# The first MLP layer's half-used products as pairs of 64 rows, and six PSUM banks in a fixed turn

## The chip, the cores and the metric

One core of a Trainium2 chip runs the whole program. The metric is the device time of one execution in microseconds. The kernel before took 1213.66 us, the median of three runs (1213.50 to 1214.83). The engines have short names in the profile: PE is TensorE (matmuls; PEld its weight loads), DVE is VectorE, ACT is ScalarE, POOL is GpSimd, and SP the engine that only issues DMAs here.

## The reference: what is computed

```
# x: 8 batches of 4224 tokens of 192 values; weight: 8 heads of 7 taps
w = softmax(weight over the 7 taps)
x = causal convolution along the tokens, 7 taps, one set of taps per head of 24 values
X = fft over tokens, then over the 192 values
u = x + real(X)
un = (u - mean(u)) / sqrt(var(u) + 1e-6)            # over the 192 values
out = u + max(un @ w_ch1, 0) @ w_ch2                # 192 -> 768 -> 192
```

All of it is fp32. The kernel carries each fp32 operand of a matmul as two fp16 parts, hi and lo, and adds three products, hi x hi, hi x lo and lo x hi.

## The kernel before, in words

**Stages.** Each batch goes through a chain of stages. `conv_unit` does the convolution with banded matrices into PSUM tiles `pc` and stores the rows to DRAM (`store_rows`); in later batches `split_windows` first makes hi and lo parts, with a small matmul `pn` for the scale. `load_x` and `split_x` bring the rows back and split them into XH and XL. `stage_a` and `stage_b` do the Fourier transform in two factors (tiles `pa` and `pb`), and `prep` the last factor (tile `pq`), which it adds to the residual `u` that `load_res` has gathered. `prep` goes on with mean, variance and normalisation, the last parts of it on GpSimd, and writes the fp16 halves `hl`. `transposes` turns `hl` into `kt` with one transposing DMA from SP. Then come the two MLP layers, `mlp_hidden` and `mlp_out`, and `store_out`.

**Steps.** The MLP works in steps of 512 tokens. A batch has nine steps, `it` 0 to 7 with 512 tokens and the short one `Q0` (`it` 8) with 128. The loop at L1127 runs over all 72 steps, numbered n. In step n it traces the hidden units of step n, the output groups of step n - 1 (four of 128 tokens), the store of step n - 2, the end of `prep` and the transpose for step n + 2, the start of `prep` for step n + 3 and gathers for n + 5. The earlier stages of the next batches are called fills. `spread` puts them evenly between these units; `stage_a` of the next batch falls into its steps `it` 3 and 4, `stage_b` mostly into 5 to 8, 0 and 1, the convolution of the batch after that into 3 to 6, and the loads and splits into 7, 8, 0, 1 and 2.

**The first layer.** The 192 inputs are 128 + 64. `W1` has four blocks of 128 rows: index 0 is the hi part of rows 0 to 127, index 1 their lo part, index 2 the hi part of rows 128 to 191, and index 3 their lo part. The 64 rows of indices 2 and 3 stand twice, in the lower and in the upper half of the partitions (`mirror_tail`). `kt` has three blocks of 128 rows: hi of 0 to 127, then hi of 128 to 191 above lo of 128 to 191, then lo of 0 to 127. For each of six tiles of 128 hidden values, L884 adds five products of 128 rows and 512 tokens:

```
order = ((0, 0), (1, 0), (0, 2), (2, 1), (3, 1))     # (block of W1, block of kt)
```

In the last, lo weights meet hi values in one half of the rows, which is needed, and lo values in the other half. L888 (ScalarE) takes relu of the tile to `hh`, and L889 (VectorE) takes the fp16 remainder to `hlo`.

**The second layer.** `mlp_out` adds 18 matmuls of 192 columns a group of 128 tokens (L903, L906, L909) into `po`, and L915 adds the result to `u`.

**PSUM.** Eight banks are three pools: tag "f" with four banks for pa, pb, pc, pq and pn, tag "h" with two for the hidden tiles `ph`, and tag "o" with two for `po`. Within a pool, a tile takes a bank that is free.

**What sets the order.** The code is written out as one stream; a planner then orders each engine's instructions ahead of time, earlier traced first among those that it takes to be ready. `after(x)` and `issue_after` put an instruction behind another on the same engine; `in_turn` puts one behind the last relu. On the chip each engine's queue keeps that order.

## Time and profile before

| | |
|---|---|
| median of three runs | 1213.66 us (1213.50 to 1214.83) |
| profiled execution, its own time | 1214.54 us |
| span of the profile, first to last instruction | 1212.7 us |
| busy PE, DVE, POOL, ACT | 1155.2, 891.5, 810.6, 637.2 us |
| mean granted clock of TensorE | 0.98 |
| chain that ended last, share of PE | 86% |

All durations come from one execution. Consecutive matmuls overlap in the records, so that their durations add up to more than the time they take; the distance from one start to the next is what counts. "Idle before" of a group is the time for which its engine did nothing just ahead of it, with what ended it.

### The profile page before, as it was taken

How to read it: one execution, taken by the hardware profiler on the slowest of the kernel's cores; microseconds unless marked ns; L12 is line 12 of the kernel's file. 1: busy time of each engine (PE TensorE's matmuls, PEld its weight loads, DVE VectorE, ACT ScalarE, POOL GpSimd, SP SyncE). 2: the span in 40 equal slices, each digit the busy share in tenths (PEclk: the TensorE clock that was granted, in tenths of full speed). 3: DMA queues.
4: the chain of work that ended last, by engine and by line, in shares of the span. 5: the costliest groups of instructions: out<-in, count | busy, mean ns of one | idle time of the engine just before them, and what ended most of it. 6: DMA issues, size and time to landing. Idle time of an engine off the chain costs nothing.

```text
span 1212.7 us, 31442 instructions
## 1 busy us (share of the span) xinstructions
PE 1155.2 (95%) x12736; PEld 913.9 (75%) x12736; DVE 891.5 (74%) x2124; ACT 637.2 (53%) x1020; POOL 810.6 (67%) x1104
## 2 busy tenths in 40 slices
PE   4279999989999999999999999999999999999998
PEld 4178768867878778787877878787787878787766
DVE  7657686787867977688777978679777887566543
ACT  5547566555655556655655655555555554333222
POOL 0217875399747897389954997479963899677940
PEclk9589999989999999999999999999999999999999
DMA  8945856366565647474663956556474643333221
GB/s 307 257 119 149 219 166 147 110 170 122 150 162 141 145 122 182 133 173 115 152 170 100 200 117 175 137 146 167 114 179 124 160 104 76 89 65 92 69 56 43
DMA packets 238370, 170.56 MB, mean 141 GB/s; under 512 B 119369, under 2 KB 221969, under 8 KB 238225
## 3 DMA queue, kind: packets, MB, share of 16 engines
q1 hardware_dynamic: 184744, 109.95, 37.3%
q10 hardware_dynamic: 46952, 45.24, 13.6%
q0 software_dynamic: 6528, 13.38, 4.4%
q8 instruction: 99, 1.62, 0.6%
q14 instruction: 47, 0.38, 0.1%
HBM read 83.82 MB, written 58.55 MB: 117 GB/s over the span
## 4 chain that ended last, share of the span: by engine, by line
PE 86%; DVE 5%; DMA 4%; ACT 2%; issue 2%; SPq 1%; ACTq 0%; another core or an unknown queue 0%; DVEq 0%
PE ph L884 33%; PE po L903 10%; PE po L909 10%; PE po L906 10%; PE pa L619 6%; PE pq L769 6%; PE pb L672 5%; PE pc L468 4%; PE pa L646 1%; DMA xs<-sc 1%; PE pc L473 1%; DMA xs_yl<-sc 1%; DMA XL<-in_w_dram 1%; ACT XH L594 1%; DVE hlo L889 1%
## 5 line engine op out<-in xcount | busy, mean ns | idle before, releaser
L884 PE MATMUL ph<-kt,W 128*128 128x512 f16 (+1 forms) x2160 | 497.7, 363 | 6.4 <-DVE hlo L889 6.3
L888 ACT ACTIVATE hh<-ph 128x512 f16<-128x512 f32 (+1 forms) x400 | 236.6, 593 | 354.7 <-PE ph L884 336.8
L909 PE MATMUL po<-W,hlo 128*128 128x192 f16 x1584 | 384.5, 246 | 0.0
L903 PE MATMUL po<-W,hh 128*128 128x192 f16 x1584 | 384.4, 246 | 0.1
L906 PE MATMUL po<-W,hh 128*128 128x192 f16 x1584 | 384.1, 246 | 0.0
L889 DVE SCALAR_TENSOR_TENSOR hlo<-ph,hh 128x512 f16<-128x512 f32 (+1 forms) x400 | 269.0, 676 | 117.6 <-ACT hh L888 114.6
L884 PEld LDWEIGHTS <-W 128*128 128x128 f16 x2160 | 192.4, 98 | 142.6 <-issue 9.4
L824 POOL TENSOR_SCALAR un<-u,mv,y 128x192 f32<-128x192 f32 x260 | 274.9, 1065 | 7.8
L718 POOL DMA_INDIRECT u<-sc,rows_sb x136 | 154.5, 1136 | 31.4 <-issue 30.8
L903 PEld LDWEIGHTS <-hh 128*128 128x128 f16 x1584 | 154.8, 98 | 24.0 <-issue 0.3
L906 PEld LDWEIGHTS <-hh 128*128 128x128 f16 x1584 | 154.7, 98 | 21.4 <-issue 0.5
L909 PEld LDWEIGHTS <-hlo 128*128 128x128 f16 x1584 | 154.8, 98 | 19.7 <-issue 0.3
L841 POOL TENSOR_TENSOR hl<-un,hl 128x512 f16<-128x512 f32 (+2 forms) x142 | 129.3, 932 | 5.6
L787 DVE SCALAR_TENSOR_TENSOR u<-pq,g,u 128x128 f32<-128x128 f32 (+1 forms) x328 | 102.9, 380 | 28.5 <-PE pq L769 24.5
L815 POOL TENSOR_SCALAR v<-mv 128x4 f32<-128x4 f32 (+1 forms) x71 | 20.1, 282 | 145.7 <-DVE mv L795 128.2
L602 DVE SCALAR_TENSOR_TENSOR XL<-xs,s_x,XH 128x768 f16<-128x768 f32 (+1 forms) x56 | 93.2, 1664 | 22.9 <-ACT XH L594 22.9
L915 DVE SCALAR_TENSOR_TENSOR u<-po,fo,u 128x384 f32<-128x384 f32 (+1 forms) x136 | 81.1, 597 | 27.0 <-PE po L909 26.9
L594 ACT ACTIVATE XH<-xs,s_x 128x768 f16<-128x768 f32 (+1 forms) x56 | 94.3, 1686 | 9.1 <-DMA xs<-sc 9.0
L769 PE MATMUL pq<-c_sb,V 128*128 128x130 f16 (+1 forms) x1440 | 96.8, 215 | 0.1
L627 ACT ACTIVATE yh<-pa 99x512 f16<-99x512 f32 x112 | 65.2, 594 | 47.2 <-PE pa L619 40.3
L769 PEld LDWEIGHTS <-V 128*128 128x128 f16 (+1 forms) x1440 | 82.2, 100 | 8.3 <-issue 2.2
L619 PE MATMUL pa<-c_sb,XH 128*128 128x128 f16 x896 | 86.5, 219 | 0.0
(158 smaller groups left out, 1740.3 us busy)
## 6 DMA issues: line engine op xcount, KB each, us to landing
out_dram<-u SPq DMA_DIRECT2D x64, 384.0 KB
xt<-in_xw_dram ACTq DMA_DIRECT2D x30, 576.0 KB
sc<-xa ACTq DMA_DIRECT2D x30, 540.0 KB
xs<-sc SPq DMA_DIRECT2D x28, 288.0 KB
u<-sc SPq DMA_DIRECT2D x72, 96.0 KB
xt<-in_xw_dram SPq DMA_DIRECT2D x10, 576.0 KB
sc<-xa SPq DMA_DIRECT2D x10, 540.0 KB
xs<-sc SPq DMA_DIRECT2D x28, 192.0 KB
```

Source lines behind the costliest of these rows:

```text
L594: split = nc.scalar.activation(part(XH), src, AF.Copy, scale=bt.c)
L619: nc.tensor.matmul(pa[:, i], x[:, at], F[:, l], start=(n == 0), stop=(n == 2))
L718: nc.gpsimd.indirect_dma_start(to, None, bt.sc[:S], bass.IndirectOffsetOnAxis(ap=rows_sb[:, col : col + 1], axis=0),)
L769: mm = nc.tensor.matmul(po, weights(v, ND * r + k3), rhs[:, 0] if it == Q0 else rhs, start=(r + n == 0), stop=(r == 1 and n == 2),)
L824: (nc.vector if b + it == 0 else nc.gpsimd).tensor_scalar(un[:, g], u[:, g], mv[:, g, 0:1], y[:, g : g + 1], op0=ALU.subtract, op1=ALU.mult,)
L841: lower = (nc.vector if b + it == 0 else nc.gpsimd).tensor_tensor(bl[:, :, o : o + n], un[:, :ng, f], hi[:, :, f], op=ALU.subtract)
L884: nc.tensor.matmul(ph[:, n], W1[:, w, ht * 128 : (ht + 1) * 128], kt[:, k], start=(i == 0), stop=(i == len(order) - 1),)
L888: anchor[0] = nc.scalar.activation(hh, ph, AF.Relu).ins
L889: nc.vector.scalar_tensor_tensor(hlo, ph, 0.0, hh, op0=ALU.max, op1=ALU.subtract)
L903: nc.tensor.matmul(po[:, g % 2], hh[:, ht, tk], W2[:, ht, 0], start=(ht == 0), stop=False)
L906: nc.tensor.matmul(po[:, g % 2], hh[:, ht, tk], W2[:, ht, 1], start=False, stop=False)
L909: nc.tensor.matmul(po[:, g % 2], hlo[:, ht, tk], W2[:, ht, 0], start=False, stop=(ht == 5),)
```

## The change

It has three parts.

1. Banks. From the first step of batch 1 on, the four banks of "f" and the two of "h" are one list of six, and each new tile takes the next bank in a fixed turn (`psum`), whether that bank is the first to come free or not. Before that step, and for "o", the old groups remain, also in turn.
2. Paired steps. In the steps of the list `PAIRED` the fifth product is left out of the five. In its place `tails` traces, ahead of the step's other units, one matmul of 64 rows for each of the six tiles, with tile 5 first: even tiles use partitions 0 to 63 of `W1` and of `kt`, odd tiles partitions 64 to 127 of `W1` and a copy of the same 64 rows of `kt` (`bt.again`). Each of the six is put behind the one before it, and the first behind the last output matmul traced so far. `mlp_hidden_full` then adds the four other products to each bank, behind the tails. The order of units in a paired step is two hidden tiles, one output group, and so on; the last output group is kept to the end of the step, after all fills.
3. The copy. `repeat_tail` is one DMA from ScalarE's queue, traced in the step before a paired one, from `kt` to upper partitions of the memory of `band`, which is not used any more by then; four places are used in turn.

```
+    bank_sets = {"f": [0, 1, 2, 3], "h": [4, 5], "o": [6, 7]}
+    def psum(shape, tag, name):
+        k = bank_sets[tag].pop(0)
+        bank_sets[tag].append(k)
+        return ps.tile(shape, F32, tag=f"bank{k}", name=name)
...
-        pa = ps.tile([128, JT, 128], F32, tag="f", name=f"pa_{b}_{t}", bufs=4)
+        pa = psum([128, JT, 128], "f", f"pa_{b}_{t}")
...
+    spare = band.rearrange("p h t -> p (h t)").bitcast(F16).rearrange(
+        "p (k g t) -> p k g t", k=4, g=4
+    )
+    def repeat_tail(bt, it):
+        to = bt.again[it] = spare[64:, (bt.b * NIT + it) % 4]
+        with in_turn():
+            nc.scalar.dma_start(to, bt.kt[it][:64, 1])
+    def tails(bt, it):
+        b = bt.b
+        bt.h[it] = (
+            sb.tile([128, 6, 512], F16, tag="hh", name=f"hh_{b}_{it}"),
+            sb.tile([128, 6, 512], F16, tag="hlo", name=f"hlo_{b}_{it}"),
+        )
+        bt.ph[it] = [psum([128, 512], "h", f"ph_{b}_{it}_{ht}") for ht in range(6)]
+        behind = last_out[0]
+        for ht, ph in reversed(list(enumerate(bt.ph[it]))):
+            at = slice(64 * (ht % 2), 64 * (ht % 2) + 64)
+            with after(behind):
+                behind = nc.tensor.matmul(
+                    ph, W1[at, 3, ht * 128 : (ht + 1) * 128],
+                    bt.again[it] if ht % 2 else bt.kt[it][at, 1],
+                    start=True, stop=False,
+                ).ins
+        bt.behind = behind
+    def mlp_hidden_full(bt, it, ht):
+        ph, kt = bt.ph[it][ht], bt.kt[it]
+        hh, hlo = (h[:, ht] for h in bt.h[it])
+        with after(bt.behind):
+            for i, (w, x) in enumerate(((0, 0), (1, 0), (0, 2), (2, 1))):
+                nc.tensor.matmul(
+                    ph, W1[:, w, ht * 128 : (ht + 1) * 128], kt[:, x],
+                    start=False, stop=(i == 3),
+                )
+        anchor[0] = nc.scalar.activation(hh, ph, AF.Relu).ins
+        nc.vector.scalar_tensor_tensor(
+            hlo, ph, 0.0, hh, op0=ALU.max, op1=ALU.subtract
+        )
+        if ht == 5:
+            del bt.ph[it], bt.again[it]
...
-            nc.tensor.matmul(
+            last_out[0] = nc.tensor.matmul(
                 po[:, g % 2], hlo[:, ht, tk], W2[:, ht, 0],
                 start=False, stop=(ht == 5),
-            )
+            ).ins
...
+    PAIRED = [
+        n for n, (bt, it) in enumerate(steps)
+        if n >= NIT and it != Q0 and (bt.b == B - 1 or it in (0, 2, 3, 4, 6) and n > NIT)
+    ]
     for n in range(len(steps) + 1):
...
+        paired = n in PAIRED
+        if paired:
+            hid = [call(mlp_hidden_full, bt, it, ht) for ht in range(6)]
         out = []
         if prev:
             out = [call(mlp_out, *prev, g) for g in range(1 if prev[1] == Q0 else 4)]
         main = []
         while hid or out:
-            if hid:
-                main.append(hid.pop(0))
-            if out:
-                main.append(out.pop(0))
+            for units in (hid, hid, out) if paired else (hid, out):
+                if units:
+                    main.append(units.pop(0))
...
+        if paired:
+            main.insert(0, call(tails, bt, it))
+        if n == NIT:
+            bank_sets["f"] = bank_sets["h"] = bank_sets["f"] + bank_sets["h"]
...
+        if n + 1 in PAIRED:
+            place([call(repeat_tail, *steps[n + 1])], 4, 1)
...
-        spread(merged, *fills)
+        keep = len(merged) - 1 if paired else len(merged)
+        closing = merged[keep:]
+        spread(merged[:keep], *fills)
+        for unit in closing:
+            unit()
```

The other places that took a PSUM tile by tag and number of buffers take it from `psum` with the same tag.

More of the change, by code (lines that the diff above doesn't have):

```diff
@@ L225, in pow2_of_norm @@
             nc.vector.tensor_reduce(tot, parts[:, :n], axis=AX.X, op=ALU.add)
-        tag, bufs = ("h", 2) if name[0] == "w" else ("f", 4)
-        pn = ps.tile([128, 512], F32, tag=tag, name=f"pn_{name}", bufs=bufs)
+        tag = "h" if name[0] == "w" else "f"
+        pn = psum([128, 512], tag, f"pn_{name}")
         nc.tensor.matmul(pn[:, :1], ones, tot, start=True, stop=True)
@@ L415, in split_windows @@
         nc.vector.tensor_scalar_max(tot, bt.nrm[:, i : i + 1], 1e-30)
-        pn = ps.tile([128, 512], F32, tag="f", name=f"pn_{bt.b}_{ch}", bufs=4)
+        pn = psum([128, 512], "f", f"pn_{bt.b}_{ch}")
         nc.tensor.matmul(pn[:, :1], ones, tot, start=True, stop=True)
@@ L441, in split_windows, with conv_unit @@
         bt.xt[ch] = (xh[:, :, :n], xl[:, :, :n], g)
-    def conv_unit(bt, ch, part, xa_slot=("xa", 2), slot=("f", 4), home=None):
+    def conv_unit(bt, ch, part, xa_slot=("xa", 2), slot="f", home=None):
         b = bt.b
@@ L459, in conv_unit @@
         n = min(3, xt.shape[2] // GRP - h0)
-        pc = ps.tile(
-            [128, 3, WC, GRP], F32, tag=slot[0], name=f"pc_{b}_{ch}_{h0}", bufs=slot[1]
-        )
+        pc = psum([128, 3, WC, GRP], slot, f"pc_{b}_{ch}_{h0}")
         with after(staged.get("pe") if b == 1 else None):
@@ L595, in split_x @@
         if bt.b == 0 and i > 3:
-            idle = ps.tile([128, HID // 3 * 2], F32, tag="h", name=f"idle_{i}", bufs=2)
+            idle = psum([128, HID // 3 * 2], "h", f"idle_{i}")
             for w in range(3):
@@ L638, in stage_a_half @@
         nj, j0 = 2 * JT, 2 * JT * t
-        pa = ps.tile(
-            [128, nj, 64], F32, tag="f", name=f"pa_0_{half}_{t}", bufs=4
-        )
+        pa = psum([128, nj, 64], "f", f"pa_0_{half}_{t}")
         cols = slice(64 * half, 64 * half + 64)
@@ L664, in stage_b @@
         for h in range(CG // CT):
-            pb = ps.tile([128, CT, 2 * NM], F32, tag="f", name=f"pb_{b}_{it}_{h}", bufs=4)
+            pb = psum([128, CT, 2 * NM], "f", f"pb_{b}_{it}_{h}")
             for i in range(CT):
@@ L747, in prep @@
         ng = 1 if it == Q0 else 4
-        pq = ps.tile([128, ND, 2, NC], F32, tag="f", name=f"pq_{b}_{it}", bufs=4)
+        pq = psum([128, ND, 2, NC], "f", f"pq_{b}_{it}")
         u = bt.u[it]
@@ L879, in mlp_hidden @@
         order = ((0, 0), (1, 0), (0, 2), (2, 1), (3, 1))
-        ph = ps.tile([128, 512], F32, tag="h", name=f"ph_{b}_{it}_{hts[-1]}", bufs=2)
+        ph = psum([128, 512], "h", f"ph_{b}_{it}_{hts[-1]}")
         ph = ph[:, : len(hts) * nt].rearrange("p (h t) -> p h t", t=nt)
@@ L891, in mlp_hidden @@
         )
+    spare = band.rearrange("p h t -> p (h t)").bitcast(F16).rearrange(
[37 more added lines that the diff above has]
+            del bt.ph[it], bt.again[it]
+    last_out = [None]
     def mlp_out(bt, it, g):
@@ L898, in mlp_out @@
         if g % 2 == 0:
-            bt.po[it] = ps.tile([128, 2, D], F32, tag="o", name=f"po_{b}_{it}_{g}", bufs=2)
+            bt.po[it] = psum([128, 2, D], "o", f"po_{b}_{it}_{g}")
         po = bt.po[it]
@@ L908, in mlp_out @@
             )
-            nc.tensor.matmul(
+            last_out[0] = nc.tensor.matmul(
                 po[:, g % 2], hlo[:, ht, tk], W2[:, ht, 0],
                 start=False, stop=(ht == 5),
-            )
+            ).ins
         if g % 2 == 1 or ng == 1:
@@ L936, in __init__ @@
             self.u, self.h, self.po, self.xs, self.xt = {}, {}, {}, {}, {}
-            self.xa = {}
+            self.xa, self.again, self.ph = {}, {}, {}
     NT = NJ // JT
@@ L1028 @@
         nc.sync.dma_start(rows_sb, rows)
-    slots = [("f", 4)] * 4 + [("h", 2)] * 2 + [("o", 2)] * 2
+    slots = ["f"] * 4 + ["h"] * 2 + ["o"] * 2
     for ch in range(NCH):
@@ L1087, in conv_chunk @@
                 second, ch, part, ("xa", 2),
-                (("h", 2), ("o", 2))[(3 * ch + part) // 2 % 2],
+                ("h", "o")[(3 * ch + part) // 2 % 2],
                 low[:, ch - 2] if ch > 1 else None,
```

## The prediction, made before the changed kernel had run

> **What bounds the kernel now.** I read the page's first parts, then its chain, then busy time by step, then TensorE's own waits.
>
> ```profile
> span 1212.7 us, 31442 instructions
> PE 1155.2 (95%) x12736; PEld 913.9 (75%) x12736; DVE 891.5 (74%) x2124; ACT 637.2 (53%) x1020; POOL 810.6 (67%) x1104
> ...
> PE 86%; DVE 5%; DMA 4%; ACT 2%; issue 2%; SPq 1%; ACTq 0%; another core or an unknown queue 0%; DVEq 0%
> PE ph L884 33%; PE po L903 10%; PE po L909 10%; PE po L906 10%; PE pa L619 6%; PE pq L769 6%; PE pb L672 5%; PE pc L468 4%; PE pa L646 1%; DMA xs<-sc 1%; PE pc L473 1%; DMA xs_yl<-sc 1%; DMA XL<-in_w_dram 1%; ACT XH L594 1%; DVE hlo L889 1%
> ```
>
> TensorE is 95% busy and 86% of the chain; one line, L884, the first layer's products, is a third of the span. The next view has the windows of single steps of batch 2 (its steps 0, 1, 2, 3, 4, 6), of step 3 of batch 7, and of step 0 of batch 1. Columns: window, length, busy time of PE, PEld, DVE, ACT, POOL, granted clock, DMA share, GB/s.
>
> ```profile
> 249.00:268.00 19.00, 15.62 (x140) 10.56 (x138) 15.55 (x37) 10.58 (x14) 17.72 (x20) 0.82 0.59 150
> ...
> 396.30:410.30 14.00, 13.83 (x152) 9.99 (x150) 13.67 (x36) 9.48 (x14) 11.27 (x16) 1.00 0.84 187
> 410.30:424.10 13.80, 13.80 (x135) 10.26 (x133) 12.32 (x27) 7.34 (x10) 12.67 (x16) 1.00 0.43 109
> 424.10:438.30 14.20, 14.20 (x131) 10.65 (x129) 10.18 (x24) 5.74 (x8) 13.00 (x18) 1.00 0.43 115
> 438.30:457.60 19.30, 19.30 (x227) 15.76 (x225) 15.32 (x38) 13.26 (x22) 17.31 (x26) 1.00 0.61 149
> 457.60:477.80 20.20, 20.20 (x246) 16.66 (x244) 16.24 (x40) 11.57 (x20) 13.92 (x18) 1.00 0.81 185
> ...
> 496.00:512.60 16.60, 16.60 (x186) 13.04 (x183) 11.62 (x36) 10.32 (x19) 1.77 (x4) 1.00 0.44 120
> ...
> 1135.50:1149.50 14.00, 14.00 (x131) 10.47 (x129) 8.12 (x23) 3.58 (x6) 13.07 (x18) 1.00 0.29 69
> ```
>
> From batch 2 on TensorE is busy in all of each step, at full clock, so a matmul fewer there shortens the step by its spacing, as long as nothing else takes over. The nearest others are VectorE in step 0 (13.67 of 14.00 us) and GpSimd in steps 1 and 2 (12.67 of 13.80, 13.00 of 14.20). Over 97 to 1213 us TensorE's waits are two rows:
>
> ```profile
> PE ph L884 <- DVE hlo L889: 6.3, 3, 3.4
> PE pc L468 <- ACT xh L435: 1.9, 1, 1.9
> ```
>
> So 8.2 us in all are waits; the rest is matmuls back to back.
>
> **What is taken away.** A paired step drops six 512-column matmuls (weight index 3, all 128 rows, half of them useful).
>
> ```profile
> 502.03 0.25 PE L903 MATMUL po<-W,hh 128*128 128x192 f16 x1
> ...
> 502.86 0.25 PE L906 MATMUL po<-W,hh 128*128 128x192 f16 x1
> 502.94 1.24 PE L884 MATMUL ph<-kt,W 128*128 128x512 f16 x5
> 504.02 0.25 PE L909 MATMUL po<-W,hlo 128*128 128x192 f16 x1
> ```
>
> Durations overlap, so I use starts: five take 504.02 - 502.94 = 1.08 us, 0.216 us each; one of the second layer's matmuls takes 502.94 - 502.86 = 0.08, more exactly 0.0825 (ten of them from 502.03 to 502.86). Removed: 6 x 0.216 = 1.296 us a step. Paired steps by the list in the code: batch 1 has 2, 3, 4, 6; batches 2 to 6 have 0, 2, 3, 4, 6; batch 7 has all eight full ones: 4 + 25 + 8 = 37.
>
> **What is added: six matmuls of 64 rows.** The trace has no 64-row matmul. The nearest thing is the only place where two matmuls use halves of the array: stage_b's first column, where L672 writes two blocks of 64 columns.
>
> ```profile
> 493.70 0.35 PE L468 MATMUL pc<-xh,halves_of_band 128*128 128x144 f16 x3
> 493.99 0.29 PE L672 MATMUL pb<-c_sb,yh 99*64 99x102 f16 x4
> 494.10 0.22 PE L672 MATMUL pb<-c_sb,yl 99*64 99x102 f16 x2
> 494.25 0.27 PE L672 MATMUL pb<-c_sb,yh 99*128 99x102 f16 x2
> ```
>
> The mean of a single one, and of the weight loads of L884, stand in the groups by line and shape (count, busy us, mean ns, idle before):
>
> ```profile
> L672 PE MATMUL pb<-c_sb,yl 99*128 99x102 f16 x504 | 76.9, 209 | 0.0
> L884 PEld LDWEIGHTS <-W 128*128 128x128 f16 x2160 | 192.4, 98 | 142.6 <-issue 9.4
> ```
>
> A single one lasts 0.209 us and the two yl together 0.22: they start about 0.01 us apart, so the halves do run side by side. I take the same for halves of rows: three pairs, 3 x 0.216 + 0.01 = 0.66 us. The bounds are this and 6 x 0.216, no overlap at all. The same rows price the change of layout. The three L468 before are 144 columns wide, 144 / 512 x 0.216 = 0.061 us each, so the next should start at 493.70 + 0.18 = 493.88 and starts at 493.99: 0.10 us lost going in. Coming out, a 102-column one should be followed 0.043 us after 494.11; it is followed at 494.25: 0.10 lost. I take 0.095 each way, 0.19 a step, if the six stay together; the code chains them, and each that another matmul separates would cost another 0.19. The bound below is zero, if a halving of rows needs no change.
>
> Saved: 1.296 - 0.66 - 0.19 = 0.446 us a step, 37 x 0.446 = 16.5 us.
>
> The Trainium skill, "TensorE: Matmul & The Clock Gate", section "Measured speedup vs the span model", gives 3.07x for four row tiles of 32 at 512 columns, not 4x. An estimate from that page, two tiles at the same share giving 1.53x, would make the six take 0.85 us and the gain 9.5 us; no trace here shows row tiles.
>
> **What is added: the wait for six banks.** The tails need all six banks at once, and the first one issued (tile 5) takes the bank handed out last, so its last reader must be done.
>
> ```profile
> L889 DVE SCALAR_TENSOR_TENSOR hlo<-ph,hh 128x512 f16<-128x512 f32 x384 | 260.2, 681 | 110.5 <-ACT hh L888 107.5 <-issue 2.0
> L888 ACT ACTIVATE hh<-ph 128x512 f16<-128x512 f32 x384 | 228.8, 597 | 343.7 <-PE ph L884 326.9 <-PE pn L417 6.4 <-issue 5.8
> ```
>
> An eviction takes 0.597 + 0.681 = 1.28 us after the last matmul. Behind the waiting tail stand on TensorE the four wide matmuls of each tile (chained behind the tails); on those wait ScalarE and VectorE, and on these the next output groups. Cover: where the step before is paired, its last output group is held to its end, 18 x 0.0825 = 1.48 us, more than 1.28. That is 19 of the 37 (steps 3 and 4 of batches 1 to 6: 12; steps 1 to 7 of batch 7: 7); cost taken zero, and if that cover were gone, 1.28 each. The other 18 follow an unpaired step: step 2 and step 6 of six batches (12), step 0 of batches 2 to 7 (6). There the planner can still put 15 of the 18 matmuls of the first output group ahead of the tails, 1.24 us against 1.28; VectorE is queued at 12.32 of 13.80 in the step before step 2. I take 0.1 us each, 1.2. At step 0 VectorE is full (13.67 of 14.00) and only one output group exists, since the step before is the short one; I take 0.5 each, 3.0. Sum 4.2 us. Bounds: 0 and 18 x 1.28 = 23.
>
> Within the step, a fill (pa, pb, pc, pq) that gets a tail's bank waits until that tile is evicted; all fills of a step must also be done before the next tails. The densest are steps 3 and 4, where VectorE has 19.30 - 15.32 = 4.0 and 4.0 us free. TensorE has 24 wide and up to 72 output matmuls there to put in between: zero, as part of the bound above.
>
> **The copy of the lower half (repeat_tail).** It is one DMA on ScalarE's queue per paired step, waiting for the transpose of that step.
>
> ```profile
> 507.60 0.32 ACTq L390 DMA_DIRECT2D sc<-xa  x1
> ...
> 410.33 1.24 PE L884 MATMUL ph<-kt,W 128*128 128x512 f16 x5
> 411.90 2.18 SPq L855 DMA_TRANSPOSE kt<-hl  x1
> 424.08 1.24 PE L884 MATMUL ph<-kt,W 128*128 128x512 f16 x5
> ```
>
> Issuing costs 0.32 us of ScalarE, which has 4 to 9 us free a step. The tightest is step 2: its transpose is issued at 411.90, 1.6 us into step 1 (410.33), and used at 424.08, 12.2 us later. The copy stands about 4/10 into step 1, near 415.8. If the transpose has not landed by then, ScalarE's next evictions queue behind the copy; paired tiles hold their own banks, so TensorE has work for a few us. Cost zero; bound 1 us at the six steps 2, 6 us. Bytes are 37 x 64 KB; no step's DMA share is above 0.84 in these windows.
>
> **Six banks in one turn, also in unpaired steps, from step 0 of batch 1 on.** The long wait of TensorE there:
>
> ```profile
> 257.30 2.29 PE L884 MATMUL ph<-kt,W 128*128 128x512 f16 x5 [3.38 <-DVE hlo L889]
> ```
>
> It waits for one of two hidden banks because VectorE is late. With six in turn it could fall away with the slow clock behind it: 3.38 + 0.18 x 15.62 = 6.2 us at most. But VectorE is as late for the other tiles, so I take zero and keep 6.2 for the range.
>
> **Sum.** The profiled run took 1214.54 us (span 1212.7 and 1.84 around it). 1214.54 - 16.5 + 4.2 = 1202.2; it lies 0.88 above the median of the runs, 1213.66, so the median forecast is 1201.4.
>
> **Rivals.**
> 1. The common turn also removes the wait of step 0 of batch 1, and bank waits are nil: 1213.66 - 16.5 - 6.2 = 1191. For: the row of 3.38 us names a hidden bank. Against: VectorE's lateness stays.
> 2. Weight loads inside the tails show. A load takes 98 ns and is hidden behind the running matmul now (0.216 spacing); if the second and third pair had to wait for theirs, 2 x 0.098 x 37 = 7.3 us go back: 1208.7. For: nothing in the full-width rows. This is where a rule speaks against the change: the Trainium skill, "TensorE: Matmul & The Clock Gate", Part 3, section "The mechanism", says that weight loads overlap running matmuls only when the row group differs; the spacing of 0.216 us in one row group, with loads of 98 ns, disagrees with it for whole-array matmuls.
> 3. Slower: the wait for the newest bank. Place: TensorE's first tail in the 18 steps after unpaired ones, behind VectorE. Price: 1.28 us each, 23 us, against 16.5: 1213.66 + 6.5 = 1220. It decides from 16.5 / 18 = 0.92 us a step on. For: VectorE at 13.67 of 14.00 in step 0. Against: 15 ready matmuls, and TensorE's present total of 8.2 us of waits.
> 4. The halves of rows do not overlap: nothing saved, 0.19 x 37 = 7 us lost: 1220.7. Against: the column halves that start 0.01 us apart.
>
> **Numbers.** Chances: forecast 0.60 (own range 1195 to 1208), rival 1 0.16, rival 2 0.08, rival 3 0.12, rival 4 0.04. The range 1191 to 1212 takes in rivals 1 and 2 and part of 3. About 0.2%, 2.4 us, is what a measurement of this kernel can tell from no change. Faster: 0.60 + 0.16 + 0.06 of rival 2 = 0.82. Same: 0.06, weak forms of 2 and 3. Slower: 0.08 of rival 3 and 0.04 of rival 4.
>
> **What would show it.** Rows of 64-row matmuls with two starts within 0.02 us, three pairs in about 0.66 us, and about 0.1 us lost on each side; paired steps shorter by 0.4 to 0.5 us (step 3 of batch 7: 14.0 to 13.55); waits of TensorE on hlo or u ahead of the tails under 0.2 us outside step 0. I am wrong if the tails are spread among other matmuls, if those waits total over 10 us, or if ScalarE waits on the copy.

## The result, and the profile after

The changed kernel takes 1229.32 us (median of 4 runs, 1227.93 to 1230.51); beside it on the same chip the kernel before takes 1214.24 us (4 runs, 1213.5 to 1215.12). The ratio is 1.0126 with an interval of 1.0112 to 1.0139: slower by 15 us, where 12 us faster was forecast. The profiled run took 1227.93 us, with a span of 1226.1 us, 13.4 us more than the 1212.7 of before.

The first lines and the chain's shares from the page of the changed kernel, which answer to the first fence of the prediction:

```profile
span 1226.1 us, 31500 instructions
PE 1149.1 (94%) x12736; PEld 900.4 (73%) x12736; DVE 887.8 (72%) x2124; ACT 641.4 (52%) x1020; POOL 814.9 (66%) x1104
...
PE 79%; DVE 7%; DMA 5%; issue 3%; ACT 2%; SPq 2%; POOL 1%; ACTq 1%; DVEq 0%; POOLq 0%
```

TensorE has less to do (1149.1 us busy against 1155.2), and its share of the chain fell from 86% to 79%. VectorE went from 5% to 7%, DMA from 4% to 5%, SyncE's queue from 1% to 2%. So the work did shrink, and the time went into waiting. TensorE's waits over the whole of the steps had two rows of 8.2 us in all; now, from 97 us to the end, there are twelve rows of 28 us in all, four of them these (line that waited, its releaser, us in total, times, longest):

```profile
PE ph L918 <- DVE V L687: 8.7, 4, 6.8
PE po L953 <- DVE u L965: 3.4, 3, 2.0
PE ph L888 <- DMA kt<-hl: 2.8, 3, 1.9
...
PE ph L918 <- DMA band<-kt: 2.0, 2, 1.2
```

L918 are the tails, the new 64-row products; L888 and L930 the other products of the first layer in unpaired and paired steps; L953, L956, L959 the second layer.

**The pairs themselves.** Step 2 of batch 3 in the timeline of the changed kernel (start, duration, engine, line, operation):

```profile
573.37 0.25 PE L956 MATMUL po<-W,hh 128*128 128x192 f16 x1
573.55 0.39 PE L918 MATMUL ph<-band,W 64*128 64x512 f16 x1
573.55 0.39 PE L918 MATMUL ph<-kt,W 64*128 64x512 f16 x1
573.78 0.38 PE L918 MATMUL ph<-band,W 64*128 64x512 f16 x1
...
574.31 1.47 PE L930 MATMUL ph<-kt,W 128*128 128x512 f16 x6
```

The two halves of a pair start at the same hundredth of a microsecond, and the next pair follows 0.22 us later. From 573.37 + 0.08, when the next matmul would have started, to 574.31 are 0.86 us (0.85 with unrounded starts): 0.66 for three pairs and 0.19 for two changes of layout, exactly the price worked out beforehand. Of the 37 paired steps 26 have their six tails together like this. In the other 11 the order written out by the planner puts other matmuls between the two halves of a pair, in ten of them between the first tail and its partner; step 3 of batch 2:

```profile
442.65 0.39 PE L918 MATMUL ph<-band,W 64*128 64x512 f16 x1
442.97 0.26 PE L953 MATMUL po<-W,hh 128*128 128x192 f16 x1
...
443.24 0.39 PE L918 MATMUL ph<-kt,W 64*128 64x512 f16 x1
443.24 0.39 PE L918 MATMUL ph<-band,W 64*128 64x512 f16 x1
...
443.68 0.38 PE L918 MATMUL ph<-kt,W 64*128 64x512 f16 x1
443.99 0.82 PE L930 MATMUL ph<-kt,W 128*128 128x512 f16 x3
```

The first and the last tail are now alone, and there are four changes of layout: 4 x 0.216 + 4 x 0.095 = 1.24 us, measured 1.27, against the 1.296 that was removed. Nothing is saved in such a step.

**Where the 13.4 us come from.** I added up TensorE's distance from each start to the next, less the spacing that the shape needs, in both traces:

| part | us against before |
|---|---|
| 37 x 1.296 removed, 26 x 0.85 and 11 x 1.27 added | -11.9 |
| waits directly ahead of or among the tails, all in steps 0, in step 3 of batch 3 and in step 6 of batches 1 and 5 | +13.1 |
| everything else, in steps and places that have no tails | +12.2 |
| span | +13.4 |

Of the 13.1 us, 10.7 are the two rows of L918 shown above. About 0.6 is the slower clock in which the six tails behind the longest of these waits run (0.40 us from pair to pair in place of 0.22), and about 1 stands in step 6 of batch 5, where an output matmul between two tails waits for VectorE (L959, 0.84 us in the view), and not a tail for a bank. Of the 12.2 us, 1.8 lie ahead of the first hidden matmul and 4.1 in batch 0.

The largest single wait is at the start of batch 6. The timelines of ScalarE, VectorE and TensorE there, in the changed kernel (in brackets the idle time before, and what ended it):

```profile
975.07 0.63 ACTq L905 DMA_DIRECT2D band<-kt  x1
975.75 1.94 ACT L600 ACTIVATE XH<-xs,s_x 128x960 f16<-128x960 f32 x1 [7.52 <-DMA kt<-hl]
...
977.71 1.84 DVE L608 SCALAR_TENSOR_TENSOR XL<-xs,s_x,XH 128x960 f16<-128x960 f32 x1 [4.94 <-ACT XH L600]
...
981.64 0.58 PE L918 MATMUL ph<-band,W 64*128 64x512 f16 x1 [6.78 <-DVE V L687]
```

ScalarE's queue stands at the copy of the lower half (L905) because the transpose of that step has not landed. Behind the copy stands a split (L600), on it VectorE's half of the split (L608), behind that the V subtraction (L687) that empties the last bank the tails need. TensorE stands 6.78 us. The transpose on the queues ahead of it, GpSimd's last part of hl and SyncE:

```profile
960.19 1.79 POOL L845 TENSOR_TENSOR hl<-un,hl 128x512 f16<-128x512 f32 x2
...
961.11 3.96 SPq L554 DMA_DIRECT2D xs<-sc  x6
965.12 0.67 SPq L716 DMA_DIRECT2D u<-sc  x1
965.90 5.14 SPq L859 DMA_TRANSPOSE kt<-hl  x1
```

hl is ready at 961.98, but six loads and a gather stand ahead on SyncE, and the transpose is issued at 965.90. The issue itself takes 5.14 us, against 2.73 for this step's transpose in the kernel before and 1.4 to 1.5 in batch 0, and the copy behind it goes out only at 975.07, 9.2 us after 965.90; why either took that long was not separated. Without the stall the tails would have begun at 981.64 - 6.78 = 974.86, 9.0 us later. In the kernel before the transpose for this step was issued at 949.96, 11.8 us ahead of the step's first product at 961.80, and no copy had to follow it.

**Loss without a single pair.** Batch 0 has no pairs, and is 4.1 us longer. By the view that gives busy time in windows (window, length, busy time of each engine, granted clock, DMA share, GB/s), from the first hidden matmul of batch 0 to that of batch 1, before:

```profile
97.32:249.06 151.74, 149.06 (x1667) 118.82 (x1665) 113.72 (x283) 89.82 (x146) 107.11 (x150) 0.99 0.62 160
```

and after:

```profile
99.11:254.94 155.83, 148.97 (x1641) 117.47 (x1639) 113.82 (x283) 88.53 (x143) 107.96 (x150) 0.99 0.56 148
```

TensorE has the same work and stands 4 us more. The SyncE queue shows why. Before:

```profile
119.93 1.43 SPq L855 DMA_TRANSPOSE kt<-hl  x1
...
126.47 0.37 SPq L928 DMA_DIRECT2D out_dram<-u  x1
...
132.33 1.45 SPq L855 DMA_TRANSPOSE kt<-hl  x1
```

After, and then on GpSimd the instruction that finishes hl for the same transposes:

```profile
127.05 0.37 SPq L978 DMA_DIRECT2D out_dram<-u  x1
127.52 1.47 SPq L859 DMA_TRANSPOSE kt<-hl  x1
...
144.18 0.37 SPq L978 DMA_DIRECT2D out_dram<-u  x1
144.64 1.53 SPq L859 DMA_TRANSPOSE kt<-hl  x1
```

```profile
119.87 1.79 POOL L845 TENSOR_TENSOR hl<-un,hl 128x512 f16<-128x512 f32 x2
...
132.29 1.78 POOL L845 TENSOR_TENSOR hl<-un,hl 128x512 f16<-128x512 f32 x2
```

hl is ready at 121.7 and 134.1, but in the new order a store of a finished step stands ahead of each transpose in SyncE's queue; the store waits until the last group of that step has been added up, and the transposes go out 5.9 and 10.6 us after hl is ready. In the kernel before these stores stood behind the transposes. What SyncE's queue waits for such additions (L965, before L915), from 99 to 260 us, before and after:

```profile
SPq L928 <- DVE u L915: 18.7, 3, 13.6
```

```profile
SPq L978 <- DVE u L965: 61.4, 5, 15.5
```

### The profile page after: what moved, and what is told of

The parts are those of the page before. It is cut to its first block, busy times and chain, and to the rows that moved or that the text cites. A ratio compares the mean times of both kernels' runs of the same rounds, so it can differ in the third digit from the quotient of the medians.

```text
span 1226.1 us, 31500 instructions
## 1 busy us (share of the span) xinstructions
PE 1149.1 (94%) x12736; PEld 900.4 (73%) x12736; DVE 887.8 (72%) x2124; ACT 641.4 (52%) x1020; POOL 814.9 (66%) x1104
## 4 chain that ended last, share of the span: by engine, by line
PE 79%; DVE 7%; DMA 5%; issue 3%; ACT 2%; SPq 2%; POOL 1%; ACTq 1%; DVEq 0%; POOLq 0%
PE ph L930 15%; PE ph L888 13%; PE po L959 9%; PE po L953 9%; PE po L956 9%; PE pa L625 6%; PE pq L773 5%; PE pc L474 4%; PE pb L676 4%; PE ph L918 3%; PE pc L479 2%; DMA xs<-sc 2%; DVE XL L608 2%; ACT XH L600 1%; DMA kt<-hl 1%
## 5 line engine op out<-in xcount | busy, mean ns | idle before, releaser
L953 PE MATMUL po<-W,hh 128*128 128x192 f16 x1584 | 386.6, 246 | 4.4 <-DVE u L965 3.4
L956 PE MATMUL po<-W,hh 128*128 128x192 f16 x1584 | 387.1, 246 | 0.0
L959 PE MATMUL po<-W,hlo 128*128 128x192 f16 x1584 | 386.1, 246 | 0.8 <-DVE wr L434 0.8
L828 POOL TENSOR_SCALAR un<-u,mv,y 128x192 f32<-128x192 f32 x260 | 289.8, 1120 | 7.8
L934 ACT ACTIVATE hh<-ph 128x512 f16<-128x512 f32 x222 | 129.3, 597 | 188.4 <-PE ph L930 169.2
L888 PE MATMUL ph<-kt,W 128*128 128x512 f16 (+1 forms) x1050 | 215.9, 345 | 6.5 <-DMA kt<-hl 2.8
L935 DVE SCALAR_TENSOR_TENSOR hlo<-ph,hh 128x512 f16<-128x512 f32 x222 | 149.1, 687 | 95.5 <-ACT hh L934 88.5
L930 PE MATMUL ph<-kt,W 128*128 128x512 f16 x888 | 204.5, 381 | 0.0
L892 ACT ACTIVATE hh<-ph 128x512 f16<-128x512 f32 (+1 forms) x178 | 103.2, 586 | 155.7 <-PE ph L888 139.0
L722 POOL DMA_INDIRECT u<-sc,rows_sb x136 | 147.6, 1085 | 31.4 <-issue 30.9
L953 PEld LDWEIGHTS <-hh 128*128 128x128 f16 x1584 | 154.8, 98 | 16.8 <-ACT hh L892 1.6
L956 PEld LDWEIGHTS <-hh 128*128 128x128 f16 x1584 | 154.8, 98 | 16.5 <-issue 5.3
L959 PEld LDWEIGHTS <-hlo 128*128 128x128 f16 x1584 | 154.5, 98 | 11.3 <-DVE wr L434 1.1
L930 PEld LDWEIGHTS <-W 128*128 128x128 f16 x888 | 83.5, 98 | 105.7 <-issue 17.4
L893 DVE SCALAR_TENSOR_TENSOR hlo<-ph,hh 128x512 f16<-128x512 f32 (+1 forms) x178 | 117.1, 669 | 49.3 <-ACT hh L892 46.0
L888 PEld LDWEIGHTS <-W 128*128 128x128 f16 x1050 | 90.2, 98 | 72.0 <-issue 6.4
L608 DVE SCALAR_TENSOR_TENSOR XL<-xs,s_x,XH 128x768 f16<-128x768 f32 (+1 forms) x56 | 92.2, 1646 | 23.6 <-ACT XH L600 22.1
L600 ACT ACTIVATE XH<-xs,s_x 128x768 f16<-128x768 f32 (+1 forms) x56 | 94.9, 1695 | 21.3 <-DMA xs<-sc 13.0
L965 DVE SCALAR_TENSOR_TENSOR u<-po,fo,u 128x384 f32<-128x384 f32 (+1 forms) x136 | 81.2, 597 | 20.5 <-PE po L959 19.2
```

Of the source, the lines that this page charges most:

```text
L608: nc.vector.scalar_tensor_tensor(part(XL), src, bt.c, part(XH), op0=ALU.mult, op1=ALU.subtract)
L722: nc.gpsimd.indirect_dma_start(to, None, bt.sc[:S], bass.IndirectOffsetOnAxis(ap=rows_sb[:, col : col + 1], axis=0),)
L828: (nc.vector if b + it == 0 else nc.gpsimd).tensor_scalar(un[:, g], u[:, g], mv[:, g, 0:1], y[:, g : g + 1], op0=ALU.subtract, op1=ALU.mult,)
L888: nc.tensor.matmul(ph[:, n], W1[:, w, ht * 128 : (ht + 1) * 128], kt[:, k], start=(i == 0), stop=(i == len(order) - 1),)
L893: nc.vector.scalar_tensor_tensor(hlo, ph, 0.0, hh, op0=ALU.max, op1=ALU.subtract)
L930: nc.tensor.matmul(ph, W1[:, w, ht * 128 : (ht + 1) * 128], kt[:, x], start=False, stop=(i == 3),)
```

## Experiments

All batch lengths below run from the first hidden matmul of a batch to that of the next (for batch 7 to the end of the span), in the profiled run of each kernel, in us. The kernels ran in three groups, each on a chip of its own and beside its own runs of the kernel before: medians 1212.42 for the first four kernels, 1205.28 for the next four, 1205.17 for the last four. The batch lengths of the kernel before are from the one trace that the prediction read.

| kernel | ratio (interval) | b0 | b1 | b2 | b3 | b4 | b5 | b6 | b7 |
|---|---|---|---|---|---|---|---|---|---|
| before | 1 | 151.7 | 147.2 | 141.5 | 141.0 | 141.0 | 142.0 | 132.5 | 118.5 |
| changed | 1.0126 (1.0112 to 1.0139) | 155.8 | 149.1 | 142.2 | 143.0 | 141.6 | 150.8 | 132.1 | 112.4 |
| e1 turn, two pools, no pairs | 1.0111 (1.0089 to 1.0133) | 155.7 | 148.8 | 141.5 | 141.5 | 141.5 | 140.1 | 137.4 | 118.5 |
| e2 turn of six, no pairs | 1.0100 (1.0073 to 1.0127) | 155.7 | 149.9 | 141.4 | 141.4 | 141.4 | 144.5 | 131.8 | 117.5 |
| e4 changed, no copy | 1.0129 (1.0104 to 1.0154) | 155.5 | 151.4 | 142.1 | 143.4 | 141.7 | 143.9 | 134.7 | 113.1 |
| e7 changed, copy on SyncE | 1.0209 (1.0179 to 1.0238) | 156.0 | 153.7 | 146.0 | 143.2 | 143.0 | 148.2 | 136.2 | 112.4 |
| e8 = e1, batch 0's stores moved | 1.0077 (1.0060 to 1.0094) | 151.7 | 148.4 | 141.4 | 141.4 | 141.4 | 140.1 | 138.9 | 118.5 |
| e11 changed, batch 0's stores moved | 1.0119 (1.0102 to 1.0136) | 151.7 | 152.2 | 142.6 | 142.1 | 141.9 | 151.0 | 132.0 | 112.4 |
| e12 = e11, pairs in 20 steps | 1.0149 (1.0132 to 1.0166) | 151.8 | 150.4 | 144.5 | 143.7 | 143.3 | 143.6 | 140.0 | 112.4 |
| e6 old pools, pairs in batch 7 | 0.9992 (0.9982 to 1.0002) | 151.6 | 146.1 | 142.3 | 141.0 | 141.0 | 141.7 | 132.6 | 117.5 |
| e3 old pools, all 37 | 1.0276 (1.0255 to 1.0298) | 151.3 | 150.9 | 147.9 | 146.7 | 146.0 | 149.5 | 136.3 | 116.8 |
| e13 = e8, pairs in batch 7 | 1.0033 (1.0023 to 1.0044) | 151.9 | 147.9 | 141.4 | 141.4 | 141.4 | 140.1 | 136.9 | 114.8 |
| e14 = e11, steps 0 unpaired | 1.0031 (1.0016 to 1.0047) | 151.9 | 148.0 | 141.3 | 141.9 | 140.5 | 143.5 | 136.2 | 112.7 |
| e15 banks of before, fixed, no pairs | 1.0124 (1.0095 to 1.0153) | 160.7 | 150.4 | 141.2 | 141.3 | 141.9 | 141.8 | 132.5 | 118.5 |

Some work moves over a batch's border when the order changes, so a single batch is compared only where nothing stands at its border, and the others in sums.

### The fixed turn alone

e1_turn_two_pools and e2_turn_six:

```
 (both)  PAIRED = []
 (e1)    # the pools of four and of two stay as they are
-        if n == NIT:
-            bank_sets["f"] = bank_sets["h"] = bank_sets["f"] + bank_sets["h"]
```

> The changed kernel without any paired step, and with the two pools kept apart: the four banks of the first pool and the two of the second are only handed out in a fixed turn. Theory A (the fixed turn itself costs time in steps that have no pairs: in the changed kernel batch 0, which has none, begins its steps 1.8 us later and lasts 4.1 us longer): about 1220 us, 5.9 more than before, with the same waits on hlo, kt and u in steps 2 to 4 of batch 0. Theory B (the loss comes from the paired steps, through the copy and the wait for six banks): 1214, as before.

> The changed kernel without any paired step, with the six banks in one turn from batch 1 on. Theory A: the six in one turn cost more than the two pools in turn, since in the changed kernel the unpaired steps 5 and 8 of batches 2 to 4 lost 0.55 and 1.65 us each against before: 1220 plus about 2 a batch for six batches, 1225 to 1232. Theory B: 1214, as before, or up to 6 us less, since the 3.4 us wait on a hidden bank in step 0 of batch 1 could go.

e1 measured 1.0111, e2 1.0100: without one pair, without one copy, the kernel is 1% slower. In size that is four fifths of the changed kernel's loss or more, though not wait for wait the same one, since the pairs win and lose time on top of it. Six banks in one turn are not better or worse than four and two. The rest of the edit costs nothing: e6 below has all of it but the turn, and pairs in the last batch alone, and its batches 0 to 6 take 996.3 us together, against 997.0 before. TensorE's waits in e1:

```profile
PE ph L888 <- DVE hlo L893: 6.7, 3, 4.5
PE po L953 <- DVE u L965: 5.7, 2, 3.5
```

The longest of each, 4.5 and 3.5 us, stand at step 0 of batch 1 and at step 0 of batch 6; batch 0 is as long as in the changed kernel. In batches 2 to 4 the turn costs at most 0.5 us each (141.5 against 141.0 to 141.5).

### The queue order in batch 0

e8_turn_sp_order puts each of batch 0's stores behind the transpose of two steps later, as it stood before; nothing else of e1 is edited. e11_after_sp_order does the same to the changed kernel:

```
+        moved[bt.b * NIT + it] = turn[0]      (in transposes)
...
     def store_out(bt, it):
         u = bt.u.pop(it)
+        k = bt.b * NIT + it
+        with after(moved.get(k + 2) if k < NIT - 2 else None):
+            store_rows_of(bt, it, u)
```

> The fixed turn in two pools, without pairs (the first experiment), and one edit: in batch 0 each store of an output is put behind the transpose of two steps later on SP's queue, as in the kernel before. Theory C (with the fixed turn the planner put the store, which waits for the last addition to u, ahead of the transpose, so that kt came 6 to 16 us later and steps 2 to 5 of batch 0 began with the store instead of with GpSimd): batch 0 loses its 4 to 5 us again, about 1221 against 1225.8. Rival (batch 0 is slower because a tile waits for its own bank while others are free): no change, 1225 to 1227.

> The changed kernel with the same edit of SP's order in batch 0. Theory C: 4 to 5 us less than the changed kernel, about 1224 to 1225. Rival: no change, 1229.

SyncE's queue in e8:

```profile
113.82 1.43 SPq L859 DMA_TRANSPOSE kt<-hl  x1
...
119.23 0.37 SPq L985 DMA_DIRECT2D out_dram<-u  x1
...
126.20 1.44 SPq L859 DMA_TRANSPOSE kt<-hl  x1
```

Batch 0 falls back to 151.7 us in e8 and in e11, its length before. So the store ahead of the transpose is shown as the cause of batch 0's 4.1 us. In e8 that reaches the total (1.0111 to 1.0077; the intervals just overlap). In e11 it does not: batch 1 grows from 149.1 to 152.2, with one wait of 3.9 us for a transpose at its step 1. The time won in one place came back as another wait.

### The same banks, fixed

e15_banks_of_before asks whether the turn hands out banks whose readers are late, or whether it is enough that the bank is named at all. Every tile gets, by name, the bank that it had in the kernel before:

```
     def psum(shape, tag, name):
+        if kept[0]:                       (true for every tile)
+            return ps.tile(shape, F32, tag=f"bank{BANKS[name]}", name=name)
...
+    PAIRED = []
```

> No pairs; every PSUM tile is given by name the very bank that it had in the kernel before, instead of any free one. So no tile changes its bank, and what is left of the change is that the bank is fixed while the order is still being written out. Theory (the order written out changes when banks are fixed, not the banks' readiness): store before transpose in batch 0 again, batch 0 at about 155.8 us against 151.7, and the whole 1.004 to 1.012. Rival (the turn hands out banks whose readers are late): with the banks of before nothing is lost, 0.998 to 1.002, batch 0 at 151.7 us.

1.0124: no better than the turn. Batch 0, in the view of windows:

```profile
89.70:250.42 160.72, 150.45 (x1641) 118.03 (x1638) 113.38 (x284) 89.09 (x146) 108.38 (x151) 0.98 0.59 143
```

and on SyncE the stores are ahead of the transposes again:

```profile
117.72 0.37 SPq L1073 DMA_DIRECT2D out_dram<-u  x1
118.18 1.50 SPq L954 DMA_TRANSPOSE kt<-hl  x1
```

No tile changed its bank, and a loss of the same size is there, though not at the same places: batches 0 and 1 are longer by 9.0 and 3.2 us, and batches 5 and 6 together are as before (274.4 us), where e1 loses 3.0 (277.5). It is the order written out that changes when banks are fixed, and with it who stands in front of whom on the queues. The rival, that the turn's banks come free later, is not needed for a loss in batches 0 and 1; for the stall of e1 at step 0 of batch 6, which e15 does not have, it is not excluded. That the planner orders differently because a tile bound to one bank becomes ready at another moment of its plan is argued; the runs show only that the same banks, fixed, give another order.

### Pairs without the fixed turn

e3_pairs_old_pools pairs all 37 steps, e6_old_pools_last the eight of the last batch, and both take any free bank, as before:

```
     def psum(shape, tag, name):
+        return ps.tile(shape, F32, tag=tag, name=name, bufs={"f": 4, "h": 2, "o": 2}[tag])
...
-        bt.ph[it] = [psum([128, 512], "h", f"ph_{b}_{it}_{ht}") for ht in range(6)]
+        bt.ph[it] = [psum([128, 512], "ffffhh"[ht], f"ph_{b}_{it}_{ht}") for ht in range(6)]
...
 (e6)    PAIRED = [n for n, (bt, it) in enumerate(steps) if it != Q0 and bt.b == B - 1]
```

> All 37 paired steps, copies included, but the PSUM banks are handed out as in the kernel before (any free bank of a pool; a paired step takes four of the pool of four and two of the pool of two). Its code order then has the six tails of a step broken up by other matmuls in 34 of the 37 steps. Theory (the pairs work, the fixed turn costs): the saving is 37 x 0.446 = 16.5 us less 0.42 us for every break that parts a pair and 0.19 for every other, some 10 us in all, and waits at the steps 0 remain, about 5 us: about the time before, ratio 0.996 to 1.003, and batch 0 (no pairs) has the length it had before, 151.7 us, not 155.8. Rival (the tails themselves cost, by waits for six banks and for the copy, whoever hands out the banks): 1.007 or more, with batches 1 to 6 each longer than before by 1 us or more.

> Pairs in the last batch alone, eight steps, and no fixed turn: the tails take four banks of the first pool and two of the second, whichever comes free. The order before the last batch is that of the kernel before. Each matmul between two tails costs up to two changes of layout of 0.095 us and a pair's overlap: by the order written out, six of the eight steps are split, by one to four other stretches. If grouping is what the fixed turn buys: 2 x 0.43 gained less about 0.2 to 0.6 for the six split ones, 1212 to 1216, no change that can be measured. If the split tails still overlap: 3.5 us less than before, about 1209.

e3 is the slowest of all, 1.0276, which I had not expected: my own theory gave 1.003 at most, and the rival (1.007 or more, batches 1 to 6 each longer) was nearer. Batch 0, as expected, has its old length (151.3), so the turn's loss is gone; but the pairs now lose: 33 of the 37 steps have their tails broken up, against 11 in the changed kernel. Step 6 of batch 3 starts so:

```profile
640.04 0.39 PE L916 MATMUL ph<-band,W 64*128 64x512 f16 x1
640.36 0.26 PE L957 MATMUL po<-W,hlo 128*128 128x192 f16 x1
...
641.37 0.39 PE L916 MATMUL ph<-kt,W 64*128 64x512 f16 x1
```

The tails are issued as their banks come free, here in three places of which the first two have one tail each, with a change of layout on both sides; this step's six cost 2.1 us in all, against 1.296 for what they replace. Over the trace the overlap of halves, less the waits between two tails, is worth 11.3 us in place of 20.7, and changes of layout cost 18.2 us more than before in place of 9.5. And the steps 0 wait for the copy:

```profile
PE ph L916 <- DMA band<-kt: 12.3, 5, 3.5
```

That is what the fixed turn is for: it keeps the tails together. e6, with tails broken up in six of eight steps, is 0.9 us shorter in the last batch and the same as before in time (0.9992). The tails give none of the 0.9: their overlap is worth 3.6 us and their changes of layout cost 3.6. It comes from the fill pq, as the smaller part does in e13 below.

### The price of a paired step, in place

e13_turn_last is e8 with six banks in turn and pairs from the first step of the last batch on; its order is that of e8 up to there.

```
-        if n >= NIT and it != Q0 and (bt.b == B - 1 or it in (0, 2, 3, 4, 6) and n > NIT)
+        if it != Q0 and bt.b == B - 1
...
-        if n == NIT:
+        if n == NIT * (B - 1):
```

> The fixed turn with the pools of four and of two until the last batch, the order of stores and transposes mended in batch 0 (as in e8_turn_sp_order), and from the first step of the last batch on six banks in turn and eight paired steps. Its code order is that of e8_turn_sp_order up to the last batch, so the two differ in that batch alone: the in-place price of eight paired steps. Theory (a paired step saves 0.446 us when its six tails stay together): three steps have a break between the halves of a pair or between pairs, so 8 x 0.446 - 2 x 0.42 - 0.19 = 2.5 us less than e8_turn_sp_order from the first matmul of the last batch to the end, and a ratio to before of about 1.0056 against 1.0077 of e8_turn_sp_order. Rival (tails bring waits for banks in every paired step, 0.3 us or more each): the last batch no shorter than in e8_turn_sp_order.

The last batch in windows, e8 and then e13:

```profile
1094.65:1213.10 118.45, 114.93 (x1084) 85.12 (x1081) 62.36 (x144) 33.07 (x58) 62.57 (x96) 1.00 0.24 63
```

```profile
1091.87:1206.67 114.80, 111.28 (x1082) 81.71 (x1080) 63.42 (x144) 33.26 (x58) 62.51 (x96) 1.00 0.27 69
```

3.65 us shorter, all of it TensorE's own work (114.93 to 111.28), and no wait of TensorE is recorded in the steps of this batch. Expected was 2.5: the six tails cost 0.85 in five steps, 1.06 in one, 1.27 in two, which is 2.5 us less than 8 x 1.296. The other 1.1 us: the 64-column matmuls of the fill pq stand apart less often in the new order, two changes of layout in place of twelve, 0.19 us in place of 1.18. The rival, a wait of 0.3 us in every paired step, has fallen for this batch, in which VectorE is busy for only 63 of 115 us. The total moved by more (1.0077 to 1.0033, some 5 us) since batch 6, whose stall at step 0 both kernels have, was 2 us shorter in this run.

### Step 0, the copy, and fewer pairs

e14_no_step0 is e11 with the steps 0 of batches 2 to 6 unpaired:

```
-        if n >= NIT and it != Q0 and (bt.b == B - 1 or it in (0, 2, 3, 4, 6) and n > NIT)
+        if n > NIT and it != Q0 and (bt.b == B - 1 or it in (2, 3, 4, 6))
```

> The changed kernel with the mended order of batch 0 (as e11_after_sp_order, which measured 1.0119), but the steps 0 of batches 2 to 6 are not paired: 32 paired steps. Theory A (the waits in front of the tails at step 0, 1.4, 0.8, 0.8, 0.8 and 6.9 us, are the price of pairing that step): they go, 10.7 us, against 5 x 0.446 = 2.2 us of saving lost, so some 8 us less, ratio 1.005. Theory B (each new order written out puts other stalls in other places; the long stall at the start of batch 6 comes with the order, not with the pair): the stall moves, ratio 1.009 to 1.014.

1.0031 against 1.0119 of e11, 10.6 us less, a little more than theory A's 8. The waits of TensorE from the start of batch 1 on:

```profile
PE ph L890 <- DMA kt<-hl: 4.4, 4, 2.3
...
PE ph L890 <- DVE V L687: 1.8, 1, 1.8
...
PE ph L920 <- DMA band<-kt: 0.8, 1, 0.8
```

The row "ph <- DVE V" of the tails is gone, in number and in length; only one wait of 0.8 us still stands ahead of a tail (L920). Pairing step 0 cost more than it could save, as theory A says. One wait that e11 has not is new, 2.3 us for a transpose at step 1 of batch 6, so theory B has a part.

e4_no_copy takes the copy out:

```
-                    bt.again[it] if ht % 2 else bt.kt[it][at, 1],
+                    bt.kt[it][at, 1],
...
-        if n + 1 in PAIRED:
-            place([call(repeat_tail, *steps[n + 1])], 4, 1)
```

> The changed kernel without the copy: the odd tiles multiply the lower 64 rows of W1 with what lies in the upper half of kt, so that their product is another one; all matmuls, banks and evictions stay. Theory B (ScalarE waits with the copy for the transpose, 7.5 us before step 0 of batch 6, and the tails wait for the copy in step 0 of batch 2 and step 3 of batch 3): 1229.3 less 6.9, 1.4 and 0.9, about 1220. Theory A (the copy is a lesser part): the gain stays under 3 us, above 1226.

The stall of 6.8 us at the start of batch 6 is gone: between 965 and 985 us one wait is left.

```profile
PE po L953 <- DVE u L965: 1.0, 1, 1.0
```

Batches 5 and 6 together take 278.6 us in place of 282.9. But the total is not better (1.0129): batch 1 is longer by 2.3 us, and the order is another one again. So the copy is shown as a link of that stall, and not as the loss as a whole.

e7_copy_sp issues the copy from SyncE instead of ScalarE:

```
-        with in_turn():
-            nc.scalar.dma_start(to, bt.kt[it][:64, 1])
+        nc.sync.dma_start(to, bt.kt[it][:64, 1])
```

> The changed kernel with the copy issued from SP's queue, behind the transposes, instead of ScalarE's. If ScalarE's wait with the copy is the cause of the stall before step 0 of batch 6, that stall of 6.9 us goes: about 1222. If SP's loads now queue behind the copy, no gain or a loss: 1228 to 1235.

1.0209, worse. SyncE's queue now stands at the copies too:

```profile
SPq L904 <- DMA kt<-hl: 81.8, 27, 5.6
```

81.8 us in all at L904, each time until a transpose has landed, with the next transposes, gathers and stores queued behind. TensorE's largest row became "ph <- DMA kt<-hl", 7.2 us.

e12_pairs_2_6_sp is e11 with pairs in steps 2 and 6 of batches 1 to 6 and in the last batch, 20 steps, of which the changed kernel had split two and seen waits in two:

```
-        if n >= NIT and it != Q0 and (bt.b == B - 1 or it in (0, 2, 3, 4, 6) and n > NIT)
+        if n > NIT and it != Q0 and (bt.b == B - 1 or it in (2, 6))
```

> The changed kernel with that edit, and pairs only in steps 2 and 6 of batches 1 to 6 and in the whole last batch: 20 paired steps, whose tails stay together on TensorE in all but two. If a paired step whose tails stay together gains 0.43 us and the rest is the fixed turn's: 1221 less 18 x 0.43 = 7.7, about 1213. If the pairs cost more elsewhere than they gain: above 1219.

Expected was the best of these kernels, measured was 1.0149, worse than e11 with 37. The tails themselves behave: no wait ahead of them in batches 3 to 5, and 0.85 us for the six where they stay together. The loss is in waits at the short step of batches 1 to 4, where no other kernel here waits more than 0.3 us for relu, and at step 1 of batches 2 to 6, where e11 has none of more than 0.3 us:

```profile
PE ph L890 <- DMA kt<-hl: 8.9, 5, 3.8
PE po L955 <- ACT hh L894: 5.3, 4, 1.7
```

Fewer pairs, another order, other stalls. With e14 (1.0031) and e12 (1.0149), which differ only in whether steps 3 and 4 are paired, the order is worth 14 us against at most 12 x 0.446 = 5.4 us that these pairs could save.

No kernel here is faster than the one before by more than a measurement can tell; the best, e6, is the same.

## Why the prediction was wrong

**The step that failed is "Six banks in one turn".** It priced the turn only from step 0 of batch 1 on, as a possible gain, and took zero. But the turn replaces "any free bank" from the first tile on, and the change alone costs 1.0% to 1.1% (e1, e2), 12 to 13 us. The reason that I gave, "VectorE is as late for the other tiles", looked at one wait on a bank; I did not ask what else the bank's name decides. It decides the order that is written out, and so the order on SyncE's, ScalarE's and GpSimd's queues: e15 loses as much with the very banks of before, though partly elsewhere, and moving batch 0's stores back (e8) returns a third of it. The section on the change had the fact, and no term of the sum answered to it. Of the 26 us between the forecast and the result, the places that have no tails, for which the sum had no term, hold 12; the wait for six banks, 13.1 in place of 4.2, holds 9, and the pairs, 11.9 in place of 16.5, hold 5.

**The pairs were right where they stay whole.** 0.66 for three pairs, 0.095 for each change of layout, 0.85 us a step: 25 of 37 steps to the hundredth once the waits ahead of them are left out, and 2.5 us for eight steps in e13, three of them split, as these prices give. That the last batch of e13 is shorter by 3.65, close to 8 x 0.446 = 3.6, is luck: 1.1 of it is the fill pq's. The 16.5 us became 11.9 because 11 steps are split. The prediction had the price of a split ("another 0.19") but left out that a split between the halves of a pair also loses their overlap, 0.216, and took none to be split since "the code chains them": the chain fixes their order, not their neighbours.

**The wait for six banks.** Zero after paired steps: right but for step 3 of batch 3 (0.78 us, for the copy). 0.1 each in steps 2 and 6 after unpaired ones: zero in ten of twelve; 0.1 in step 6 of batch 1, and about 1 in step 6 of batch 5, which is an output matmul's wait. 0.5 each in the six steps 0: measured 1.3, 0.7, 0.7, 0.7, 6.8 and 0. The place, VectorE at the full step 0, was right, and so was the usual size; in batches 3 to 6 the bank that is late is that of a fill (pb, whose reader is the V subtraction), not one of the hidden ones; in batch 2 it is the copy. The bound of 1.28 us a step was broken, since it counted one eviction as late and not a queue behind a queue.

**The copy.** Taken as zero, bound 1 us at the steps 2. Its rows there hold. What happened was at step 0 of batch 6, where the transpose was issued 9.0 us ahead of its use in place of 11.8, and the copy passed the lateness on to ScalarE's split, VectorE and the tails: 6.8 us, gone in e4. That "paired tiles hold their own banks, so TensorE has work for a few us" was not so at a step whose tails had not yet started.

**The rivals.** 1: with six banks in turn the wait of 3.38 us for a hidden bank is gone, but at its place a pq tile waits 2.53 us for VectorE (4.1 in e2) and step 1 waits 1.88 us for its transpose, and batch 1 is longer (149.1 us against 147.2). So "VectorE's lateness stays" was right; e1, with two hidden banks, waits 4.5 there. 2: weight loads in the tails are hidden, at 0.22 us from pair to pair. This stands against the rule of the Trainium skill, "TensorE: Matmul & The Clock Gate", Part 3, section "The mechanism", that loads overlap running matmuls only when the row group differs, for row halves too: the loads of the second pair go to the same two halves that the first pair is computing in, and their records begin 0.01 us behind its start (573.56 against 573.55). 4: false, the halves overlap fully. The estimate from the Trainium skill, the same page, section "Measured speedup vs the span model" (no full overlap), is not borne out at 512 columns: two halves give 2.0 times. 3 had the sign and, in step 0, the place: with its 18 steps and 1.28 us it would have given 23 us; the tails' waits were 13.1, and e14 shows that leaving step 0 unpaired takes some 10 us off. But that is half of what was lost, and the other half had no rival at all.

The signs that were named for being wrong, splits among other matmuls, waits over 10 us ahead of the tails, ScalarE waiting on the copy, have all three come, the second (10.7 us) with waits for the V subtraction and the copy and not, as named, for hlo or u.

**What stays open.** In profiled runs the kernels e13 and e14 take from their first hidden matmul to the end 1115.8 and 1115.9 us (1206.67 - 90.91, 1207.16 - 91.22), as the kernel before does (1212.73 - 97.32 = 1115.4). Yet their ratios are 1.003, some 4 us. Where these stand is open. A longer stretch ahead of the first hidden matmul is not shown: e3, which takes any free bank as the kernel before does, has that matmul at 90.22 us, and e13 and e14 of the same group have it at 90.91 and 91.22. The trace of the kernel before is from runs of 1213.66 us, and beside e13 and e14 that kernel takes 1205.17, so its lengths cannot be set beside theirs to a few us. Nor did I find which of the planner's choices makes the stalls of steps 0 of batches 1 and 6; that they move with every edit is shown, what moves them isn't.

## What to carry to other kernels

Where a planner writes out the order, whatever ties a buffer to a name can be an edit to every queue, also in stretches that the change doesn't touch: price it by running that part alone before the part that is meant to gain. A gain of half a microsecond a step, on an engine that is busy all the time, is soon lost by stores that stand ahead of transposes (4.1 us in batch 0); look in the trace at what each in-order queue (SyncE's above all) has at its head while TensorE waits. And half-array products pay only if partners are issued back to back: a pair that is parted costs 0.216 us of overlap and 0.19 us of layout, nearly all of the 0.446 us that its step could save.

## What the runs showed of the hardware

Two 64-row products on the two halves of the array start 3 to 6 ns apart and take the time of one: 0.22 us from pair to pair at 512 columns, as for one product of 128 rows. A change of layout between 128 rows and 64 costs 0.096 us going in and 0.092 coming out, the same as between 128 columns and 64 (0.10 by the rows that the prediction quotes). Both were expected by analogy and not seen before in this kernel. Not expected was how a wait travels: at the start of batch 6 four queues stood one behind the other, SyncE's transpose, ScalarE's copy, VectorE's subtraction and TensorE's tail, and each showed only the one before it as its releaser. Behind that stall of 6.78 us TensorE's granted clock was 0.51 for 3.4 us (981.64 to 985.00).
